# Block-sparse attention and rational FFN: weight remainders subtracted on VectorE instead of GpSimd, and unit factors in one operation

## The chip, the core and the metric

The program runs on one core of a Trainium2 chip. The metric is the device time of one execution in microseconds. Three runs of the kernel before took 829.0, 827.88 and 829.31 us; their median is 829.0 us. Engines are called as in the profile: PE is TensorE (matmuls), DVE is VectorE, ACT is ScalarE, POOL is GpSimd, SP is SyncE.

## The reference, cut to what matters

```
# attention: batch 4, 8 heads, 768 positions in 24 blocks of 32, head_dim 64; a query block sees its
# neighbours, the first and last block, and three sampled blocks
attn = softmax(where(mask, q @ k.T / 8, -1e9));  x = (attn @ v) as (3072, 512)
# feed-forward: 512 -> 2048 -> 512; the weights w_in and w_out come as float64
h = x @ w_in
P = a[0] + a[1]*h + a[2]*h**2 + a[3]*h**3
Q = 1 + abs(b[0])*abs(h) + abs(b[1])*h**2
out = (P / (Q + 1e-6)) @ w_out
```

## The kernel before, in words

Attention goes over parts (a batch and a pair of query blocks): scores on PE (tile `m`), maxima on DVE (L829), exponentials on ACT (L848), transposes of the weights on PE (L894), values on PE (`av`), and the result, scaled, as a float16 pair `xh`, `xl`. The feed-forward part takes 256 rows of x at a time (a chunk) and 256 of the 2048 hidden columns at a time (a unit): PE multiplies into `ph` (L1036 to L1038), ACT and DVE evaluate the rational function (`sq`, `tt`, `ab`, `rr`; L1043 to L1081) up to `gh` and `gl`, and PE multiplies these with w_out into `acc` (L1093 to L1099).

The weights come in double precision and are turned into pairs of low-precision numbers on the chip, in about the first 215 us. A piece of w_out is loaded (`wl`), converted (`dw`, helper line L154 on POOL, L150 on ACT), packed by three DVE instructions (L441, L444, L447), rounded to its high part `wo_h`, and its low part `wo_l` is the difference of both: L461, 16 pieces of 128x512. A piece of w_in takes the same three packing steps, then a scale (`dw<-wi,scw`), a rounding to float16, and its low part is again a difference: L519, 16 pieces. For each group of units four factors are computed (`fc`, L1010: the scale of the group times 1, |b0|, a1 and a3), by four small operations; there are 7 groups in the kernel, four of them in the stretch of the weights.

The order of all instructions on all engines is computed in Python before the program runs: each step is an `Op` with an engine (or several that it may use, in `among`), a price in ns, what it waits for, and a due time. `issue` repeatedly picks the step that can start first by these prices. Each engine then executes its list strictly in that order and waits for semaphores on the way, so a wait holds everything that stands behind it. Where PE would idle early on, `issue` puts in matmuls on an identity matrix (`fill`, L162).

A piece's rounding (`wo_h`, key "o") and conversion may go to ACT, POOL or DVE as the planner finds them free; a w_in remainder ("l") could go to POOL alone, a w_out remainder ("p") to POOL or DVE.

Of the kernel before, what the change touches and what calls it, by code (L numbers as in the profile page):

```python
# [24 lines left out]
def kernel(  # L25
# [27 lines left out]
    nc = tc.nc  # L53
# [233 lines left out]

    par = const.tile([P, 8], F32, name="par")
    absb = const.tile([P, 2], F32, name="absb")
    bias = const.tile([P, NB, NS], F32, name="bias")  # L290

    def load_small():
# [4 lines left out]
    def setup():  # L297
        nc.vector.tensor_scalar(out=ix, in0=samp[0:1].rearrange("p i (n w) -> p i n w", w=2)[:, :, :, 0],
                                scalar1=0, scalar2=NB - 1, op0=ALU.max, op1=ALU.min)
        nc.scalar.activation(out=absb, in_=par[:, 4:6], func=AF.Abs)  # L300

        sf = work[:, 2 * NR * NB:3 * NR * NB].rearrange("p (n i) -> p n i", n=NR)
        nc.vector.tensor_copy(out=sf, in_=samp.rearrange("p i (n w) -> p n i w", w=2)[:, :, :, 0])
        ii = work[:, 5 * NR * NB:5 * NR * NB + NB]
        nc.gpsimd.iota(ii, pattern=[[1, NB]], base=0, channel_multiplier=0, allow_small_or_imprecise_dtypes=True)
        dup = work[:, 3 * NR * NB:4 * NR * NB].rearrange("p (n i) -> p n i", n=NR)
        tmp = work[:, 4 * NR * NB:5 * NR * NB].rearrange("p (n i) -> p n i", n=NR)
        for r in range(NR):
            nc.vector.tensor_tensor(out=dup[:, r], in0=sf[:, r], in1=ii, op=ALU.subtract)
        nc.vector.tensor_tensor(out=dup, in0=dup, in1=dup, op=ALU.mult)  # L310
        nc.vector.tensor_scalar(out=dup, in0=dup, scalar1=1.0, scalar2=None, op0=ALU.is_le)
        for edge in (0.0, NB - 1.0):
            nc.vector.tensor_scalar(out=tmp, in0=sf, scalar1=edge, scalar2=None, op0=ALU.is_equal)
            nc.vector.tensor_tensor(out=dup, in0=dup, in1=tmp, op=ALU.max)
        for r in range(1, NR):
            for e in range(r):
                nc.vector.tensor_tensor(out=tmp[:, r], in0=sf[:, r], in1=sf[:, e], op=ALU.is_equal)
                nc.vector.tensor_tensor(out=dup[:, r], in0=dup[:, r], in1=tmp[:, r], op=ALU.max)
        nc.vector.memset(bias, 0.0)
        nc.vector.memset(bias[:, 1, NR:NR + 1], NEG)  # L320
        nc.vector.memset(bias[:, NB - 2, 1:2], NEG)
        for r in range(NR):
            for e in range(2):
                nc.vector.tensor_scalar(out=bias[:, 1 - e:NB:2, r + 5 * e], in0=dup[:, r, 1 - e:NB:2], scalar1=NEG, scalar2=None, op0=ALU.mult)
# [72 lines left out]
    def weights():  # L397
# [21 lines left out]
        def one(prio, kind, u, x, before):  # L419
            d = {}  # L420
            s_wl = Slot(r_wl) if kind else None
            s_w = Slot(r_dw) if kind else None

            def load():
                d["ld"] = early.tile([P, 2 * WC], I32, name="wl", bufs=2) if kind else raw(u, x)
                if kind:
                    nc.sync.dma_start(out=d["ld"], in_=wo64[x * P:(x + 1) * P])
                    return
                r0 = head(x, 0) * D
                if u == 0 and x == 0:  # L430
                    nc.gpsimd.tensor_copy(out=d["ld"][:, 0:1].bitcast(F32), in_=kall[:, 12, 0, 0:1])
                (nc.sync if u > 1 else nc.gpsimd).dma_start(out=d["ld"], in_=wi64[r0:r0 + P, u * 2 * WC:(u + 1) * 2 * WC])

            def convert(eng):
                d["w"] = early.tile([P, WC], I32, name="dw", bufs=3) if kind else wi[:, x, u].rearrange("p a n -> p (a n)").bitcast(I32)
                d["words"] = d["ld"].rearrange("p (n w) -> p n w", w=2)
                times(eng, d["w"].bitcast(F32), d["words"][:, :, 1].bitcast(F32), 2.0 ** -112)

            def pack1():
                w = d["w"]  # L440
                nc.vector.tensor_scalar(out=w, in0=w, scalar1=3, scalar2=None, op0=ALU.logical_shift_left)  # L441

            def pack2():
                nc.vector.scalar_tensor_tensor(out=d["w"], in0=d["words"][:, :, 0], scalar=29, in1=d["w"], op0=ALU.logical_shift_right, op1=ALU.bitwise_or)  # L444

            def pack3():
                nc.vector.scalar_tensor_tensor(out=d["w"], in0=d["words"][:, :, 1], scalar=-2 ** 31, in1=d["w"], op0=ALU.bitwise_and, op1=ALU.bitwise_or)  # L447

            def most():
                if u not in sums:  # L450
                    sums[u] = early.tile([P, 8], F32, name="sums")
                bound(d["w"].bitcast(F32), sums[u][:, x:x + 1])

            def out_high(eng):
                times(eng, wo_h[:, x], d["w"].bitcast(F32), 1.0)

            def out_short(eng):
                times(eng, wo_b[:, x], d["w"].bitcast(F32), 1.0)

            def out_low(eng):  # L460
                eng.tensor_tensor(out=wo_l[:, x], in0=d["w"].bitcast(F32), in1=wo_h[:, x].bitcast(F32), op=ALU.subtract)  # L461

            wl = [s_wl] if kind else []
            if kind or u > 1:
                o0 = Op(SY, [(475, 524288)], load, [o_setup] if kind else [freed[u - 1, x]], prio - 2, takes=wl, behind=before[kind])
            else:
                o0 = Op(PO, [(700, 524288)], load, [k_evac[0][3]] if u == 0 else [begun[0, x]], -17.0 + 1.2 * x if u else -84, behind=before[kind])
            before[kind] = o0
            w = [s_w] if kind else []
            o = Op(among("c", SC, sc=520, po=588, ve=335), 0, convert, [o0], prio, takes=w, uses=wl)  # L470
            if not kind:
                begun[u, x] = o
            o = Op(VE, 335, pack1, [o], prio, uses=w)
            o = Op(VE, 602, pack2, [o], prio, uses=wl + w)
            o = Op(VE, 602, pack3, [o], prio, uses=wl + w)
            if not kind:
                freed[u, x] = o
            if kind:
                o1 = Op(among("o", SC, sc=520, po=588, ve=335), 0, out_high, [o], prio, uses=w)
                o2 = Op(among("p", PO, po=1225, ve=602), 0, out_low, [o1] + homes(x), prio, uses=w)  # L480
                o3 = Op(among("q", SC, sc=520, po=588, ve=335), 0, out_short, [o] + homes(x), prio, uses=w)
                out_ready[x] = [o2, o3]
                decoded.append(o3)
                decoded.append(o2)
                return o2
            return Op(SC, 613, most, [o], prio)
# [9 lines left out]
    def w_scaled(u, prio, group, sums):  # L496
# [10 lines left out]
        for x in range(NCC):  # L507
            def three(x):
                d, s_ws = {}, Slot(r_dw)

                def scaled(eng):
                    d["w"] = early.tile([P, WC], I32, name="dw", bufs=3).bitcast(F32)
                    times(eng, d["w"], wi[:, x, u].rearrange("p a n -> p (a n)").bitcast(F32), sc[0])

                def high(eng):
                    times(eng, wi[:, x, u, 0], d["w"], 1.0)

                def low(eng):
                    eng.tensor_tensor(out=wi[:, x, u, 1], in0=d["w"], in1=wi[:, x, u, 0], op=ALU.subtract)  # L519

                a = Op(among("s", PO, po=671, ve=396, sc=613), 0, scaled, [o], prio, takes=[s_ws])
                a = Op(among("h", SC, sc=520, po=588, ve=335), 0, high, [a], prio, uses=[s_ws])
                a = Op(among("l", PO, po=1113, ve=602), 0, low, [a], prio, uses=[s_ws])
                in_ready.setdefault(u, []).append(a)
                decoded.append(a)
            three(x)
# [477 lines left out]
    def factors(b, u, n, after, prio):  # L1004

        def run():
            if b not in fcs:
                fcs[b] = p2.tile([P, 4, NU], F32, name="fc")
            for j, coef in enumerate((1.0, absb[:, 0:1], par[:, 1:2], par[:, 3:4])):
                nc.vector.tensor_scalar(out=fcs[b][:, j, u:u + n], in0=wscale[:, u:u + n], scalar1=v_inv[b], scalar2=coef, op0=ALU.mult, op1=ALU.mult)  # L1010
        for x in range(u, u + n):
            o_fc[b, x] = None
        o = Op(VE, 700, run, after + [o_fc.get((b, 0))], prio)
        for x in range(u, u + n):
            o_fc[b, x] = o

# [229 lines left out]
```

## Time and profile before

| | |
|---|---|
| median of three runs | 829.0 us |
| the profiled execution | 828.6 us, its span 826.8 us |
| PE busy | 770.6 us (93%) |
| DVE busy | 674.9 us (82%), 1580 instructions |
| ACT busy | 569.7 us (69%) |
| POOL busy | 107.5 us (13%), 149 instructions, all before 216 us |
| mean granted TensorE clock | 0.983 |

Busy time is the time in which at least one instruction of the engine is in execution. The span is the time from the first to the last instruction. The profile cuts the span into 40 slices of 20.7 us and gives the busy share of each engine in tenths:

```profile
PE   8798918898999999999999999999999999999997
DVE  2788999899988885788878884887888886887886
POOL 3547485613100000000000000000000000000000
PEclk9999969899999999999999999999999999999999
```

The sixth slice (103 to 124 us) is the one place where PE is nearly idle (1), and where its granted clock fell (6).

### The profile page before, as it was taken

What the parts mean: (1) busy time and instruction counts of PE and PEld (TensorE: products, weight loads), DVE (VectorE), ACT (ScalarE), POOL (GpSimd) and SP (SyncE); (2) the same over time, 40 slices, a digit from 0 to 9 for tenths busy, and PEclk for the clock granted to TensorE, in tenths of its full rate; (3) what the DMA queues carried; (4) which work ended last, traced back from release to release, by engine and by line L of the source; (5) the groups of instructions that cost most, each with busy time, mean ns of one, the idle gap of its engine ahead of it and who ended that gap; (6) DMA issues with size and microseconds to landing.
All of it is one profiled execution on the core that took longest, in us unless ns stands there. A gap on an engine that the chain in (4) does not pass through costs nothing.

```text
span 826.8 us, 27468 instructions
## 1 busy us (share of the span) xinstructions
PE 770.6 (93%) x10859; PEld 557.3 (67%) x10943; DVE 674.9 (82%) x1580; ACT 569.7 (69%) x1264; POOL 107.5 (13%) x149
## 2 busy tenths in 40 slices
PE   8798918898999999999999999999999999999997
PEld 4556605676677768677777767677777767767774
DVE  2788999899988885788878884887888886887886
ACT  2676777677866769677576759676676758766563
POOL 3547485613100000000000000000000000000000
PEclk9999969899999999999999999999999999999999
DMA  7988874537566957545636757635555436220000
GB/s 210 242 220 238 233 231 138 163 87 189 142 154 165 214 162 194 162 123 162 160 108 164 191 145 196 173 96 157 144 151 149 117 111 182 76 65 2 1 26 26
DMA packets 224416, 121.29 MB, mean 147 GB/s; under 512 B 62624, under 2 KB 214048, under 8 KB 224288
## 3 DMA queue, kind: packets, MB, share of 16 engines
q1 hardware_dynamic: 223136, 115.34, 51.6%
q0 software_dynamic: 1152, 4.19, 1.6%
q8 instruction: 86, 1.41, 0.8%
q14 instruction: 42, 0.34, 0.1%
HBM read 108.47 MB, written 11.01 MB: 145 GB/s over the span
## 4 chain that ended last, share of the span: by engine, by line
PE 81%; DVE 7%; DMA 4%; issue 3%; ACT 2%; POOL 2%; SPq 1%; ACTq 0%; POOLq 0%; DVEq 0%
PE acc L1093 11%; PE ph L1036 9%; PE acc L1095 9%; PE acc L1099 9%; PE ph L1037 9%; PE ph L1038 9%; PE m L817 7%; PE av L940 6%; PE m L894 6%; PE acc L162 3%; DMA vg<-in_v_dram 2%; PE m L556 2%; DMA wl<-in_moe_w_out_dram 1%; PE m L978 1%; POOL wo_h L154 1%
## 5 line engine op out<-in xcount | busy, mean ns | idle before, releaser
L1037 PE MATMUL ph<-xl,wi 128*128 128x256 f16 x768 | 210.5, 274 | 3.1 <-DVE xl L989 3.1
L1036 PE MATMUL ph<-xh,wi 128*128 128x256 f16 x768 | 210.9, 275 | 1.4 <-DVE tt L1053 1.4
L1038 PE MATMUL ph<-xh,wi 128*128 128x256 f16 x768 | 210.7, 274 | 0.0
L1043 ACT ACTIVATE sq<-ph,fc 128x512 f32<-128x512 f32 x96 | 65.9, 687 | 112.6 <-PE ph L1038 112.4
L1093 PE MATMUL acc<-wo_h,gh 128*128 128x512 f32 x384 | 114.5, 420 | 18.7 <-DVE gh L1071 18.0
L848 ACT ACTIVATE pr<-pr,st 128x256 f32<-128x256 f32 x224 | 110.7, 501 | 14.3 <-DVE st L860 14.3
L1060 DVE SCALAR_TENSOR_TENSOR ab<-sq,absb,ab 128x512 f32<-128x512 f32 x96 | 73.2, 763 | 37.1 <-ACT ab L1057 36.9
L829 DVE CUSTOM_DVE_ANT_1 pr<-m,bias 128x256 f32<-128x256 f32 x224 | 83.2, 418 | 22.3 <-PE m L817 22.1
L1099 PE MATMUL acc<-wo_b,gl 128*128 128x512 bf16 x368 | 95.4, 379 | 3.4 <-issue 2.1
L1095 PE MATMUL acc<-wo_l,gh 128*128 128x512 bf16 x316 | 86.5, 384 | 4.6
L1036 PEld LDWEIGHTS <-wi 128*128 128x128 f16 x768 | 75.9, 99 | 21.4 <-issue 5.1
L1071 DVE SCALAR_TENSOR_TENSOR gh<-tt,par,rr 128x512 fp32r<-128x512 f32 x96 | 72.3, 753 | 19.8 <-ACT rr L1067 11.2
L1093 PEld LDWEIGHTS acc<-wo_h,gh 128*128 128x128 f32 x384 | 66.0, 191 | 32.7 <-issue 19.6
L150 ACT ACTIVATE pT<-m 128x512 f32<-128x512 f32 x112 | 64.1, 596 | 34.0 <-PE m L894 32.7
L1037 PEld LDWEIGHTS <-wi 128*128 128x128 f16 x768 | 75.6, 98 | 12.7 <-issue 0.2
L1038 PEld LDWEIGHTS <-wi 128*128 128x128 f16 x768 | 75.5, 98 | 12.6 <-issue 3.4
L1047 ACT ACTIVATE tt<-ph,par,fc 128x512 f32<-128x512 f32 x96 | 74.8, 779 | 0.3 <-DVE gl L1081 0.2
L1050 DVE TENSOR_TENSOR tt<-tt,sq 128x512 f32<-128x512 f32 x96 | 66.9, 697 | 9.4 <-ACT tt L1047 9.4
L1057 ACT ACTIVATE ab<-ph,fc 128x512 f32<-128x512 f32 x96 | 65.6, 683 | 11.2 <-DVE tt L1077 10.5
L1077 DVE SCALAR_TENSOR_TENSOR tt<-tt,par,ab 128x512 f32<-128x512 f32 x96 | 72.2, 752 | 0.5
L894 PE MATMUL m<-ident,pr 128*128 128x128 f32 x448 | 69.6, 288 | 2.9 <-ACT kt L150 2.3
L1053 DVE SCALAR_TENSOR_TENSOR tt<-ph,fc,tt 128x512 f32<-128x512 f32 x96 | 71.4, 744 | 0.8
(130 smaller groups left out, 1221.7 us busy)
## 6 DMA issues: line engine op xcount, KB each, us to landing
vg<-in_v_dram SPq DMA_DIRECT2D x312, 64.0 KB, 2.9
vg<-in_v_dram SPq DMA_DIRECT2D x88, 192.0 KB, 3.6
kall<-ks SPq DMA_DIRECT2D x138, 64.0 KB, 1.9
wl<-in_moe_w_out_dram SPq DMA_DIRECT2D x16, 512.0 KB, 4.8
vg<-in_v_dram SPq DMA_DIRECT2D x12, 512.0 KB, 5.1
kall<-ks SPq DMA_DIRECT2D x23, 256.0 KB, 3.7
ldq<-in_q_dram SPq DMA_DIRECT2D x20, 256.0 KB, 3.4
out_dram<-ld SPq DMA_DIRECT2D x20, 256.0 KB, 2.4
```

Source lines behind the costliest of these rows:

```text
L829: nc.vector.tensor_tensor_reduce(out=prs[x][:, e, g].rearrange("p (s r) -> p s r", r=BLK), in0=h["sp"][g][:, e], in1=add.rearrange("p (s o ...
L848: nc.scalar.activation(out=prs[x][:, e, g], in_=prs[x][:, e, g], func=AF.Exp, scale=SCALE, bias=st[:, 12 + y:13 + y], accum_out=st[:, 16 + ...
L894: nc.tensor.transpose(pp[:, jj * P:(jj + 1) * P], pr[:, e, g, kt:NS * BLK:2], ident)
L1036: nc.tensor.matmul(o, wh, xh[:, :, cc], start=(cc == 0), stop=False)
L1037: nc.tensor.matmul(o, wh, xl[:, :, cc], start=False, stop=False)
L1038: nc.tensor.matmul(o, wl, xh[:, :, cc], start=False, stop=(cc == NCC - 1))
L1047: nc.scalar.activation(out=d["tt"], in_=d["ph"], func=AF.Identity, scale=d["cst"][:, 3:4], bias=par[:, 2:3])
L1060: nc.vector.scalar_tensor_tensor(out=d["ab"], in0=d["sq"], scalar=absb[:, 1:2], in1=d["ab"], op0=ALU.mult, op1=ALU.add)
L1071: nc.vector.scalar_tensor_tensor(out=d["gh"], in0=d["tt"], scalar=par[:, 0:1], in1=d["rr"], op0=ALU.add, op1=ALU.mult)
L1093: nc.tensor.matmul(acc, g, wo_h[:, f], start=(new and e == 0), stop=False)
L1095: nc.tensor.matmul(acc, g, wo_l[:, f], start=False, stop=False)
L1099: nc.tensor.matmul(acc, g, wo_b[:, f], start=False, stop=(last and e == 1))
```

## The change

The w_in remainder ("l") and the w_out remainder ("p") are given to DVE alone, priced at 602 ns each. The four small operations that make a group's factors become one `scalar_tensor_tensor` over four coefficients and n units; the four coefficients are gathered once, in the setup, into a tile `coefs` by a memset and three copies of one column, the first of which reads what ACT has just written (`absb`). The price of the step falls from 700 to 180 ns. Five lines are added, so that L461 of before is L466 after, L519 is L524, L441/L444/L447 are L446/L449/L452, and L1071 (`gh`) is L1076.

```
+    coefs = const.tile([P, 4], F32, name="coefs")
...
         nc.scalar.activation(out=absb, in_=par[:, 4:6], func=AF.Abs)
+        nc.vector.memset(coefs[:, 0:1], 1.0)
+        nc.vector.tensor_copy(out=coefs[:, 1:2], in_=absb[:, 0:1])
+        nc.vector.tensor_copy(out=coefs[:, 2:3], in_=par[:, 1:2])
+        nc.vector.tensor_copy(out=coefs[:, 3:4], in_=par[:, 3:4])
...
-                o2 = Op(among("p", PO, po=1225, ve=602), 0, out_low, [o1] + homes(x), prio, uses=w)
+                o2 = Op(among("p", VE, ve=602), 0, out_low, [o1] + homes(x), prio, uses=w)
...
-                a = Op(among("l", PO, po=1113, ve=602), 0, low, [a], prio, uses=[s_ws])
+                a = Op(among("l", VE, ve=602), 0, low, [a], prio, uses=[s_ws])
...
-            for j, coef in enumerate((1.0, absb[:, 0:1], par[:, 1:2], par[:, 3:4])):
-                nc.vector.tensor_scalar(out=fcs[b][:, j, u:u + n], in0=wscale[:, u:u + n], scalar1=v_inv[b], scalar2=coef, op0=ALU.mult, op1=ALU.mult)
+            nc.vector.scalar_tensor_tensor(out=fcs[b][:, :, u:u + n], in0=coefs.rearrange("p (j o) -> p j o", o=1).broadcast_to([P, 4, n]), scalar=v_inv[b],
+                                           in1=wscale[:, u:u + n].rearrange("p (o u) -> p o u", o=1).broadcast_to([P, 4, n]), op0=ALU.mult, op1=ALU.mult)
...
-        o = Op(VE, 700, run, after + [o_fc.get((b, 0))], prio)
+        o = Op(VE, 180, run, after + [o_fc.get((b, 0))], prio)
```

The whole order is planned anew with these prices. Counted over the program's order, DVE executes 32 remainders instead of 1, 7 factor operations instead of 28, and 7 fewer conversions, scalings and roundings (`dw<-wi,scw` 4 to 1, `dw<-wl` 2 to 0, `wo_h` 2 to 1, `wi<-wo_l` 2 to 1). POOL loses all of its 31 remainders and takes these 7 (43 operations of L154 instead of 36). ACT's number does not change, nor does the number of fill matmuls (135).

The first place is DVE's list where the first factors and the first `xl` are made (about 52 to 57 us of the trace before). Before:

```order
L344 TENSOR_REDUCE sc_1035<-m_101 128x1
L347 TENSOR_SCALAR sc_1035<-sc_1035 128x1
L351 TENSOR_SCALAR sc_1035<-sc_1035 128x1
L355 TENSOR_SCALAR sc_1035<-sc_1035 128x1
L356 TENSOR_SCALAR sc_1035<-sc_1035 128x1
L660 COPY xscale<-sc_1035 128x1
L1010 TENSOR_SCALAR fc<-wscale,sc_1035 128x2
L1010 TENSOR_SCALAR fc<-wscale,sc_1035,absb 128x2
L1010 TENSOR_SCALAR fc<-wscale,sc_1035,par 128x2 x2
```

After, the same stretch (`sc` is the scale of the values of the first batch, on which `xscale` and `xl` hang):

```order
L349 TENSOR_REDUCE sc_1040<-m_102 128x1
L524 TENSOR_TENSOR wi<-dw,wi 128x512
L352 TENSOR_SCALAR sc_1040<-sc_1040 128x1
L524 TENSOR_TENSOR wi<-dw,wi 128x512
L356 TENSOR_SCALAR sc_1040<-sc_1040 128x1
L524 TENSOR_TENSOR wi<-dw,wi 128x512
L360 TENSOR_SCALAR sc_1040<-sc_1040 128x1
L361 TENSOR_SCALAR sc_1040<-sc_1040 128x1
L971 TENSOR_TENSOR xn<-av,st 128x256
L665 COPY xscale<-sc_1040 128x1
L524 TENSOR_TENSOR wi<-dw,wi 128x512
```

The four remainders of the first group of w_in now stand between the steps of the scale; the single factor operation and both `xl` follow them.

The second place is DVE's list just ahead of the third `gh`, the one for which PE waited longest before. Before:

```order
L444 SCALAR_TENSOR_TENSOR dw<-wl,dw 128x512
L1050 TENSOR_TENSOR tt<-tt,sq 128x512
L447 SCALAR_TENSOR_TENSOR dw<-wl,dw 128x512
L1060 SCALAR_TENSOR_TENSOR ab<-sq,absb,ab 128x512
L1071 SCALAR_TENSOR_TENSOR gh<-tt,par,rr 128x512
```

After:

```order
L452 SCALAR_TENSOR_TENSOR dw<-wl,dw 128x512
L874 TENSOR_TENSOR st<-st 128x4
L452 SCALAR_TENSOR_TENSOR dw<-wl,dw 128x512
L877 TENSOR_SCALAR st<-st 128x4
L1055 TENSOR_TENSOR tt<-tt,sq 128x512
L880 RECIPROCAL st<-st 128x4
L466 TENSOR_TENSOR wo_l<-dw,wo_h 128x512
L1076 SCALAR_TENSOR_TENSOR gh<-tt,par,rr 128x512
L466 TENSOR_TENSOR wo_l<-dw,wo_h 128x512
```

Two w_out remainders stand now directly ahead of and behind this `gh`; the rounding `wo_h` that each of them needs is made on POOL.

The third place is POOL's list where it works on w_out pieces (101 to 122 us before). Before:

```order
L154 TENSOR_SCALAR wo_h<-dw 128x512
L461 TENSOR_TENSOR wo_l<-dw,wo_h 128x512
L154 TENSOR_SCALAR wo_h<-dw 128x512
L461 TENSOR_TENSOR wo_l<-dw,wo_h 128x512
L154 TENSOR_SCALAR dw<-wl 128x512 x2
L154 TENSOR_SCALAR wi<-wo_l 128x512
L461 TENSOR_TENSOR wo_l<-dw,wo_h 128x512 x2
L154 TENSOR_SCALAR dw<-wl 128x512
```

After:

```order
L154 TENSOR_SCALAR wo_h<-dw 128x512
L154 TENSOR_SCALAR wi<-wo_b 128x512
L154 TENSOR_SCALAR wo_h<-dw 128x512
L154 TENSOR_SCALAR dw<-wl 128x512
L154 TENSOR_SCALAR wo_h<-dw 128x512
L154 TENSOR_SCALAR dw<-wl 128x512
L154 TENSOR_SCALAR wo_h<-dw 128x512
L154 TENSOR_SCALAR dw<-wl 128x512
```

Nothing but operations with one input tensor is left on POOL there.

## Rows read from the trace of the kernel before

**Rows 1.** Busy time by stretch (us), instructions in brackets, clock, DMA.

```profile
core 0: us, PE busy (x) PEld busy (x) DVE busy (x) ACT busy (x) POOL busy (x), PEclk, DMA share, GB/s
50.00:225.00 175.00, 139.55 (x2342) 100.81 (x2352) 163.60 (x377) 126.85 (x288) 89.75 (x94) 0.92 0.64 180
109.60:126.60 17.00, 4.51 (x13) 2.81 (x14) 15.23 (x25) 11.23 (x26) 10.67 (x9) 0.50 0.63 204
225.00:800.00 575.00, 566.65 (x7658) 416.50 (x7728) 463.60 (x1068) 406.54 (x890) 0.00 (x0) 1.00 0.50 135
```

**Rows 2.** PE's waits, 46 to 230 us: us in total, times, longest.

```profile
PE acc L1093 <- DVE gh L1071: 18.0, 2, 17.6
PE ph L1037 <- DVE xl L989: 3.1, 1, 3.1
```

**Rows 3.** Chain of waits, 100 to 125 us: start, us, what.

```profile
101.42 7.89 POOL wo_h L154
...
109.39 1.58 POOL wo_l L461
...
121.28 0.67 DVE gh L1071
```

**Rows 4.** POOL's groups: count, busy us, mean ns, idle before.

```profile
L461 POOL TENSOR_TENSOR wo_l<-dw,wo_h 128x512 bf16<-128x512 f32 x15 | 22.5, 1503 | 13.5 <-ACT wo_h L150 11.7 <-DVE wo_h L152 1.1
L519 POOL TENSOR_TENSOR wi<-dw,wi 128x512 f16<-128x512 f32 x16 | 19.6, 1247 | 5.2 <-ACT wi L150 5.2
```

**Rows 5.** DVE in order of time: start, us, instruction, idle before it.

```profile
38.95 0.43 DVE L872 TENSOR_SCALAR st<-st 128x4 f32<-128x4 f32 x1
...
52.99 0.66 DVE L1010 TENSOR_SCALAR fc<-wscale,sc 128x2 f32<-128x2 f32 x1
...
101.98 0.42 DVE L441 TENSOR_SCALAR dw<-dw 128x512 int32<-128x512 int32 x1
102.31 0.68 DVE L1081 TENSOR_TENSOR gl<-tt,rr 128x512 bf16<-128x512 f32 x1
102.92 0.68 DVE L444 SCALAR_TENSOR_TENSOR dw<-wl,dw 128x512 int32<-128x512 int32 x1
...
109.76 1.75 DVE L444 SCALAR_TENSOR_TENSOR wi<-wo_b,wi 128x512 int32<-128x512 int32 x1
...
114.55 0.87 DVE L441 TENSOR_SCALAR dw<-dw 128x512 int32<-128x512 int32 x1 [1.77 <-POOL dw L154]
...
208.91 0.83 DVE L441 TENSOR_SCALAR dw<-dw 128x512 int32<-128x512 int32 x1
...
215.16 1.08 DVE L1077 SCALAR_TENSOR_TENSOR tt<-tt,par,ab 128x512 f32<-128x512 f32 x1
```

**Rows 6.** DVE in order of time at the third batch's factors.

```profile
398.86 0.23 DVE L1010 TENSOR_SCALAR fc<-wscale,sc 128x8 f32<-128x8 f32 x1
398.99 0.28 DVE L1010 TENSOR_SCALAR fc<-wscale,sc,absb 128x8 f32<-128x8 f32 x1
...
399.57 0.68 DVE L1074 SCALAR_TENSOR_TENSOR ab<-ab,gh 128x512 f32<-128x512 f32 x1
```

**Rows 7.** DVE's waits, 46 to 230 us.

```profile
DVE dw L154 <- POOL wi L519: 2.0, 1, 2.0
DVE dw L441 <- POOL dw L154: 2.0, 2, 1.8
DVE dw L154 <- POOL wo_l L461: 1.4, 1, 1.4
```

**Rows 8.** POOL in order of time: a rounding to `wo_h` that shares its time with DVE.

```profile
142.12 1.04 POOL L154 TENSOR_SCALAR wo_h<-dw 128x512 fp32r<-128x512 f32 x1
```

**Rows 9.** ACT's `absb`, then DVE in order of time, in the setup.

```profile
5.26 0.20 ACT L300 ACTIVATE absb<-par 128x2 f32<-128x2 f32 x1 [3.23 <-DMA par<-in_moe_b_dram]
...
4.54 0.26 DVE L303 CAST rr<-rr 128x72 f32<-128x72 int32 x1
...
11.65 0.69 DVE L152 COPY kall<-ph 128x512 f32<-128x512 f32 x1 [2.50 <-PE ph L556]
```

## The prediction

> **What bounds the kernel now.** I read the busy time by stretch first. From 225 to 800 us PE is busy 566.65 of 575 us at full clock; POOL does nothing there. From 50 to 225 us, while the weights are decoded, PE is busy for only 139.55 of 175 us and DVE for 163.60 [rows 1]. So whatever the change is worth, it is worth it before 225 us, and it reaches the end if PE, which has little air later, starts its steady part earlier or later by it.
>
> PE's waits say which engine ends its idle time there: 18.0 us for `gh` from DVE, of which one wait is 17.6, and 3.1 for `xl`, also from DVE [rows 2]. The chain of waits through that long wait runs over POOL, an engine that is 13% busy in the whole: a rounding to `wo_h` of 7.89 us, a remainder `wo_l` of 1.58, and at the end DVE's `gh` [rows 3]. The timeline of DVE shows why: at 109.76 an L444 took 1.75 us, while the one at 102.92 took 0.68, and POOL's remainder that began at 109.39 lay beside the long one; and at 114.55 DVE had been idle 1.77 us for a conversion on POOL [rows 3, 5]. I take from this that the two engines hold each other up, both ways: DVE's run of operations from 101.98 on kept POOL's 7.89 us operation waiting, and POOL's remainders lengthen DVE's.
>
> The Trainium skill has a rule for it ("SBUF — State Buffer", section "Who interferes with whom"): a DVE instruction with two SBUF inputs or in a two-port mode and a GpSimd instruction that reads SBUF exclude each other, and the later one is blocked for the whole of the earlier. These rows agree. By the rule alone the remainders could cost DVE up to their whole 42.1 us on POOL; the count below gives less than half of it, since DVE often had PSUM work or stood idle.
>
> **The change part by part.** All terms are DVE time between 50 and 225 us, where DVE is what PE waits for.
>
> Remainders: POOL loses 15 of 1503 ns and 16 of 1247 ns [rows 4], and DVE gains 31. On DVE a 128x512 operation on two tensors in SBUF takes its place in the list for 0.60 us: 102.31 to 102.92 is 0.61 [rows 5]. 31 x 0.60 = +18.6 us. Bound from below 0.60, and from above 0.75 each (+23) if the roundings beside them block some.
>
> What DVE gets back: I counted each DVE instruction that ran over 60 ns longer than the short value of its form, and put the excess down to the POOL instruction that overlapped it most. 27 belong to L461 and L519, the first at 52.99 and the last at 215.16 [rows 5], and sum to 19.4 us. 24 belong to POOL's 36 conversions, scalings and roundings (L154), the first at 38.95 and the last at 208.91 [rows 5], and sum to 9.6 us. So -19.4 from the remainders. Bounds: nothing, if other POOL work steps into the same places, and -19.4 - 9.6 = -29 if all of it goes.
>
> Moved conversions: DVE loses 7 of 0.33 us (101.98 to 102.31 [rows 5]): -2.3. POOL's L154 operations go from 36 to 43; at 9.6 / 36 = 0.27 us of DVE time each, 7 more cost +1.9.
>
> Factors: a group of four took 398.86 to 399.57 = 0.71 us where POOL was silent [rows 6]. The single operation over the broadcast coefficients is not in the trace; it lies between 0.13 us (the step from 398.86 to 398.99 [rows 6]) and 0.60 (a 128x512 one). With 8 elements a partition it is near the small one: 0.2. Four groups in this stretch: -0.5 x 4 = -2.0 (-0.4 to -2.3). Their blocked time is already in the 19.4. The three later groups stand where PE bounds: nothing.
>
> Setup: DVE must now wait for `absb`, which ACT ends at 5.46, instead of going on at 4.54, and does four small copies: some 1.3 us later. DVE then stands idle 2.50 us before the copy at 11.65 [rows 9]; that cover takes it. Without it the cost is 1.3.
>
> DVE's work together: 18.6 - 19.4 - 2.3 + 1.9 - 2.0 = -3.2 us.
>
> Waits that go: DVE waited 2.0 us for L519 and 1.4 for L461, and 1.8 for a conversion that stood behind remainders in POOL's list [rows 7]: -5.2.
>
> Waits that come: ten of the `wo_l` remainders on DVE need a `wo_h` that POOL makes. Where DVE's list between packing and remainder holds only work with its inputs in SBUF, as from 101.98 us on before, POOL may not get to start until DVE stops at the remainder. In DVE's list this is so, or nearly, for six of the ten. A rounding that shares its time with DVE takes 1.04 us [rows 8]; half of it, six times: +3.1. Bounds 0 and 10 x 1.04 = 10.4. Behind such a remainder stand `gh`, `ab` and `tt` of the next unit, and PE for them. The 16 w_in remainders wait for ACT's rounding; POOL waited 5.2 us in the same place [rows 4]. DVE has other work planned in between; I take +1.0, with 0 and 5.2 as ends.
>
> Sum: -3.2 - 5.2 + 3.1 + 1.0 = -4.3 us. The profiled execution took 828.6 us, of which the span is 826.8 and 1.8 lies around it; 828.6 - 4.3 = 824.3. The median of the runs is 829.0, 0.4 above it, so I put 824.5.
>
> **The rivals.**
>
> Ordered waits on DVE (slower). The remainders no longer sit in a queue of their own but in the list of the engine PE waits for, so each late rounding on POOL or ACT holds up the whole rational function behind it. For it: two remainders stand directly ahead of and behind the third `gh`, each behind a POOL rounding, and one such rounding took 7.89 us [rows 3]. Against it: when DVE stops, POOL has the memory to itself, so a wait ends within about 1 us. What I gain without any new wait is 3.2 + 5.2 = 8.4 us; from 8.4 us of waits on this is slower. At its ends, 10.4 + 5.2 = 15.6, it gives 828.6 + 7.2 = 835.8; in the middle between this and the turning point 832.
>
> A saturated engine (slower). The stall time is not given back, since other POOL work fills it, and only 18.6 - 2.3 - 2.0 = +14.3 remains: 843. The Trainium skill ("Perfetto Trace Analysis", section "Optimizing Scalar/DVE Operations") advises to move work from a saturated DVE to ScalarE or even GpSimd, the opposite of this change, but adds that between DVE and GpSimd it might not help, because they share a port. This trace bears out the second half: the 42.1 us on POOL cost DVE 19.4 plus 3.4 of waiting, more than the 18.6 that the same work costs there.
>
> No new waits (much faster). If DVE's list is such that the roundings are always ready, the 3.1 + 1.0 are not paid: -8.4. The clock may then stay up too: the stretch from 109.60 to 126.60 has a granted clock of 0.50, the lower of the two levels (1.2 GHz), having fallen while PE stood idle in its wait of 17.6 us, and PE is busy 4.51 us in it [rows 1, 2]; at 2.4 GHz half of this, 2.3, would come back: 828.6 - 8.4 - 2.3 = 817.9. Against it: the DVE work ahead of the third `gh` is hardly less than before, so PE idles there again.
>
> No change. PE's work is the same, and the relief of DVE may only lengthen its own idle time: 139.55 us of PE and 126.85 of ACT must also run through this stretch [rows 1]. Then 828 to 830. For it: the two orders run alike from the later batches on, where PE sets the pace. Against it: nearly all of PE's idle time before ends on DVE.
>
> **How the numbers follow.** A change of less than 0.2% (1.7 us) cannot be told from none here. Forecast, a gain of 2 to 9 us: 0.45. No new waits: 0.15. No change: 0.13. Ordered waits: 0.21. Saturated: 0.06. So faster 0.60, same 0.13, slower 0.27. The likeliest case alone reaches from 820 to 827; 8 in 10 lie between 815 and 834, which takes in most of the case without new waits and of the ordered waits.
>
> **What would show it.** If the step is right: DVE's busy time from 50 to 225 us is a few us lower or the stretch shorter by as much; L872, L441 and the two-input operations have means near those without POOL; 32 remainders on DVE at about 0.6 to 0.7 us; each `fc` operation near 0.2 us; PE's long wait for `gh` is there but some 4 to 6 us shorter; from 225 us on nothing differs. Wrong would be: DVE's waits on POOL's `wo_h` and ACT's `wi` together above 8 us (the ordered waits), or L154's means on POOL and DVE's excess beside them grown as much as the remainders' went (saturated). If the time falls below 818, the clock will show no low stretch near 110 to 127 us.

## The result, and the profile after

Four runs of the changed kernel have a median of 839.34 us, against 829.15 for four of the kernel before on the same chip: 1.0122 times, 95% interval 1.0106 to 1.0138. It is slower by 10 us; forecast were 824.5, and 834 as the upper end. The profiled execution took 839.82 us, its span 837.7.

The page of the changed kernel; busy time, then busy tenths in 40 slices of 20.9 us:

```profile
PE 783.8 (94%) x10943; PEld 559.9 (67%) x10943; DVE 668.2 (80%) x1587; ACT 570.9 (68%) x1264; POOL 65.3 (8%) x125
...
PE   7898755799899999999999999999999999999997
...
DVE  2688699889898886778877875787887886888886
...
POOL 3335134310000000000000000000000000000000
PEclk9999898699999999999999999999999999999999
```

POOL lost 42 us of busy time and DVE 7. PE's one empty slice (the 1 of before) has become four poor ones, 5 to 8, and the lowest clock stands two slices later. (The larger busy time of PE is not more work: the trace of before has 84 records of PE fewer.)

By stretch [rows 1]:

```profile
core 0: us, PE busy (x) PEld busy (x) DVE busy (x) ACT busy (x) POOL busy (x), PEclk, DMA share, GB/s
50.00:225.00 175.00, 138.83 (x2259) 97.61 (x2258) 152.10 (x376) 121.44 (x274) 47.69 (x70) 0.90 0.67 175
225.00:800.00 575.00, 572.93 (x7830) 417.14 (x7829) 462.60 (x1071) 410.40 (x902) 0.00 (x0) 1.00 0.57 137
```

DVE has 11.5 us more air in the stretch of the weights, and PE does no more in it, at a lower mean clock. The DMA engines are busier (0.67 for 0.64, and 0.57 for 0.50 later) at fewer or hardly more GB/s.

PE's waits, 46 to 230 us [rows 2]: what was waited for, us in total, times, longest.

```profile
PE m L344 <- ACT kt L150: 7.9, 1, 7.9
PE m L983 <- DVE st L834: 5.8, 1, 5.8
PE ph L1041 <- DVE tt L1058: 5.1, 4, 3.3
PE av L945 <- DMA vg<-in_v_dram: 4.8, 2, 3.5
...
PE m L561 <- DMA ldq<-in_q_dram: 1.8, 1, 1.8
PE acc L1098 <- DVE gh L1076: 1.3, 2, 1.0
```

The 17.6 us for `gh` are gone. In their place stand a wait of 7.9 for ACT, one of 5.8 for DVE, 3.3 for `tt`, and waits for two DMAs that before had none of this size. By the starts of the 96 `gh` operations, the changed kernel is 2.4 us late at the first (88 us before), between 5.1 and 11.1 from the second to the 16th, where the two orders differ, and between 10.3 and 10.7 from 248 us to 449. All of the loss arises before 248 us, and the steady part keeps its pace.

DVE's groups after [rows 4], then its waits, 46 to 230 us [rows 7]:

```profile
L466 DVE TENSOR_TENSOR wo_l<-dw,wo_h 128x512 bf16<-128x512 f32 x16 | 11.8, 737 | 1.3 <-POOL wo_h L154 1.3
L524 DVE TENSOR_TENSOR wi<-dw,wi 128x512 f16<-128x512 f32 x16 | 11.3, 726 | 2.2 <-ACT wi L150 2.1
L446 DVE TENSOR_SCALAR dw<-dw 128x512 int32<-128x512 int32 x16 | 6.9, 444 | 4.6 <-POOL dw L154 3.7 <-ACT dw L150 0.9
L1014 DVE SCALAR_TENSOR_TENSOR fc<-coefs,sc,wscale 128x8 f32<-128x8 f32 (+1 forms) x7 | 2.3, 323 | 0.0
```

```profile
DVE xn L971 <- PE av L945: 6.6, 4, 4.2
DVE pr L834 <- PE m L822: 6.2, 5, 2.4
DVE dw L446 <- POOL dw L154: 3.7, 2, 2.5
DVE wi L524 <- ACT wi L150: 2.1, 3, 0.9
DVE wo_l L466 <- POOL wo_h L154: 1.3, 3, 0.5
```

The remainders cost about what was forecast and hardly wait for their roundings. DVE now waits for PE, not PE for DVE alone. Nothing in DVE's own rows is worth 10 us, so the cause had to be looked for elsewhere.

Where PE first takes up a tile of q, in the setup. Before:

```profile
12.14 0.66 PE L556 MATMUL m<-ident,ldq 128*128 128x128 f32 x4
```

After:

```profile
14.22 0.66 PE L561 MATMUL m<-ident,ldq 128*128 128x128 f32 x4 [2.43 <-DMA ldq<-in_q_dram]
```

And the DMA row of the same time, what all queues moved in 40 slices of 0.4 us from 0 to 16 us. Before:

```profile
GB/s 0 0 0 0 30 49 49 37 17 8 62 194 291 286 285 273 287 270 207 210 261 289 286 263 271 235 260 284 271 277 228 108 13 0 96 96 165 180 236 353
```

After:

```profile
GB/s 0 0 0 0 29 50 49 35 17 11 58 204 288 287 255 217 218 218 207 223 222 199 213 228 227 220 219 215 219 219 219 231 168 158 122 179 201 184 236 297
```

Both start alike up to the 14th slice. Then the loads of k and q, which no edit touches, run at 263 GB/s before and 220 after, in the mean of the 15th to the 28th slice. The six tiles of k, 256 KB each in pieces of 256 bytes, land 0.91 us apart before (four of the five steps; one is 1.31) and 1.20 after (all five).

### The profile page after: what moved, and what is told of

Same layout as the page of the kernel before. It is cut to its first block, busy times and chain, and to the rows that moved or that the text cites. A ratio compares the mean times of both kernels' runs of the same rounds, so it can differ in the third digit from the quotient of the medians.

```text
span 837.7 us, 27545 instructions
## 1 busy us (share of the span) xinstructions
PE 783.8 (94%) x10943; PEld 559.9 (67%) x10943; DVE 668.2 (80%) x1587; ACT 570.9 (68%) x1264; POOL 65.3 (8%) x125
## 4 chain that ended last, share of the span: by engine, by line
PE 83%; DMA 5%; DVE 4%; SPq 2%; ACT 2%; issue 2%; POOL 1%; POOLq 0%; ACTq 0%; DVEq 0%
PE acc L1098 11%; PE ph L1041 10%; PE acc L1104 10%; PE acc L1100 10%; PE ph L1042 10%; PE ph L1043 10%; PE m L822 7%; PE av L945 6%; PE m L899 6%; DMA vg<-in_v_dram 3%; PE acc L162 2%; PE m L561 2%; PE m L983 1%; DMA ldq<-in_q_dram 1%; SPq L586 1%
## 5 line engine op out<-in xcount | busy, mean ns | idle before, releaser
L853 ACT ACTIVATE pr<-pr,st 128x256 f32<-128x256 f32 x224 | 110.7, 501 | 10.3 <-DVE st L865 10.3
L1100 PE MATMUL acc<-wo_l,gh 128*128 128x512 bf16 x384 | 101.2, 386 | 0.0
L1104 PE MATMUL acc<-wo_b,gl 128*128 128x512 bf16 x384 | 98.7, 379 | 2.0 <-DVE gl L1086 2.0
L1076 DVE SCALAR_TENSOR_TENSOR gh<-tt,par,rr 128x512 fp32r<-128x512 f32 x96 | 72.3, 754 | 20.9 <-ACT rr L1072 12.3
L1062 ACT ACTIVATE ab<-ph,fc 128x512 f32<-128x512 f32 x96 | 65.5, 683 | 13.4 <-DVE tt L1082 12.8
```

The lines of the kernel that those rows point to most:

```text
L853: nc.scalar.activation(out=prs[x][:, e, g], in_=prs[x][:, e, g], func=AF.Exp, scale=SCALE, bias=st[:, 12 + y:13 + y], accum_out=st[:, 16 + ...
L1076: nc.vector.scalar_tensor_tensor(out=d["gh"], in0=d["tt"], scalar=par[:, 0:1], in1=d["rr"], op0=ALU.add, op1=ALU.mult)
L1100: nc.tensor.matmul(acc, g, wo_l[:, f], start=False, stop=False)
L1104: nc.tensor.matmul(acc, g, wo_b[:, f], start=False, stop=(last and e == 1))
```

## The experiments

Theories at the start. T1: the remainders are cheaper on DVE, as forecast, and the order that is planned anew with their prices is at fault. T2: the remainders in DVE's list are at fault. T3: the setup's wait for `absb` delays the start. A fourth came from the DMA rows. T4: `coefs`, 16 bytes in a slot of 32, shifts all SBUF tiles behind it by 32 bytes, and loads to the shifted addresses are slower. In the built programs `tt` (k is loaded there first) lies at 153600 before and 153632 after, `vg0` at 114688 and 114720, `ldq` at 143360 and 143392: multiples of 256 before, 32 above one after.

Each ratio below is to the kernel before, run beside it on the same chip.

**ctrl: before, unchanged.**

> The kernel before, unchanged, profiled once more. It tells how far the first 50 us vary with nothing changed. In the profile before, the k tiles landed 0.9 us apart and PE idled 7.3 us in the first 50 us; in the changed kernel's profile 1.2 us apart and 10.6 us. If the start is a matter of the change (theory: the setup's wait for absb), this run lands the tiles 0.9 us apart again and PE idles 7 to 8 us; if it varies by itself, the steps lie between 0.9 and 1.2 us. Time 828 to 831 either way.

Measured: 828.55 us, 1.0003 (0.9989 to 1.0017). The same kernel under another name agrees within 0.2%.

**planB_dve: the order of before, the remainders executed by DVE.** The planner still takes them for POOL's; PE, ACT and SP have the lists of before word for word.

```
-                eng.tensor_tensor(out=wo_l[:, x], ...
+                nc.vector.tensor_tensor(out=wo_l[:, x], ...
-                    eng.tensor_tensor(out=wi[:, x, u, 1], ...
+                    nc.vector.tensor_tensor(out=wi[:, x, u, 1], ...
```

> The order of before on PE, ACT and SP word for word, and its factors; but the 31 remainders that stood in POOL's list are executed by DVE, at the place where the planner put them out. Theory 1 (the remainders are cheaper on DVE than the hold-ups they caused on POOL; the loss comes from the new order, in which PE's waits fall so that its clock is low while it works): faster than before by 2 to 7 us, 822 to 827. Theory 2 (the remainders in DVE's list hold up what stands behind them, whatever the order): slower than before by 5 to 12 us, 834 to 841.

Measured: 825.88 us, 0.9963 (0.9946 to 0.998), the first version that is faster, by 0.4%. DVE where before ran from 102.31 to 114.55 us [rows 5]:

```profile
101.51 0.69 DVE L461 TENSOR_TENSOR wo_l<-dw,wo_h 128x512 bf16<-128x512 f32 x1 [0.51 <-POOL wo_h L154]
102.12 0.68 DVE L1081 TENSOR_TENSOR gl<-tt,rr 128x512 bf16<-128x512 f32 x1
...
111.52 0.68 DVE L444 SCALAR_TENSOR_TENSOR wi<-wo_b,wi 128x512 int32<-128x512 int32 x1
...
113.38 0.41 DVE L441 TENSOR_SCALAR dw<-dw 128x512 int32<-128x512 int32 x1
```

Its longest wait of PE [rows 2], in the list of waits:

```profile
PE acc L1093 <- DVE gh L1071: 18.3, 2, 15.7
```

The L444 of 1.75 us now takes 0.68, and the L441 that stood idle 1.77 us for POOL does not wait (another L441, at 86.11 us, now waits 1.81 for a conversion on POOL; before it was 0.23); the remainder at 101.51 waits 0.51 us for its rounding; PE's wait falls from 17.6 to 15.7. T2 falls: in the same order the remainders are better off on DVE.

**planA_pool: the order of after, the remainders executed by POOL.** The same two lines in the changed kernel, with `nc.gpsimd`; the planner takes them for DVE's.

> The order of the changed kernel on PE, ACT and SP word for word, and its single factor operation; but the 32 remainders are executed by POOL at the place where the planner put them out. Theory 1 (the order is at fault): no better than the changed kernel, 839 to 848, since the hold-ups of DVE by POOL come back (some 19 us of DVE time). Theory 2 (DVE's list is at fault): near the kernel before, 827 to 833.

Measured: 840.43 us, 1.014 (1.0123 to 1.0157). All of the loss is there with no remainder on DVE.

**coefs_late: the four coefficient operations at the end of the setup.**

```
-        nc.vector.memset(coefs[:, 0:1], 1.0)
-        nc.vector.tensor_copy(out=coefs[:, 1:2], in_=absb[:, 0:1])
...
+        (the four lines as the last of setup)
```

> The changed kernel with the four operations that fill coefs moved to the end of the setup, so that DVE does not wait for absb at 4.5 us. Theory 3 (the setup's wait delays the start and with it everything): PE's first scores come 1 to 4 us earlier than in the changed kernel and the time falls by 1 to 4 us, 835 to 838. Theories 1 and 2: no change that can be told, 837.5 to 841.

Measured: 840.71 us, 1.0138 (1.01 to 1.0175). No gain, so T3 falls. The setup of the changed kernel, DVE in order of time [rows 9], says the same:

```profile
5.64 0.15 DVE L303 COPY coefs<-absb 128x1 f32<-128x1 f32 x1 [1.06 <-ACT absb L301]
...
11.40 0.69 DVE L152 COPY kall<-ph 128x512 f32<-128x512 f32 x1 [0.94 <-PE ph L561]
```

The wait of 1.06 us is there; the idle time before the copy shrinks from 2.50 to 0.94 and the copy stands no later than before.

**before_shift32: before, with an unused tile of 16 bytes.**

```
     absb = const.tile([P, 2], F32, name="absb")
+    pad = const.tile([P, 4], F32, name="pad")
```

> The kernel before, instruction for instruction, with one more 16-byte constant tile that nothing uses, allocated where the change puts coefs. It shifts the SBUF address of every tile behind it by 32 bytes, as coefs does: the k, q and v tiles (tt, ab, sq, ldq, vg) then no longer start at a multiple of 256 bytes. Theory 4 (the shifted addresses make these loads slower, and that is what costs the time): the k tiles land 1.2 us apart instead of 0.9, the median landing of the 64 KB v loads goes from 2.9 to 3.8 us, and the time rises by 6 to 12 us, to 835 to 841. Theory 1 (the new order is at fault): no change, 827 to 831.

Measured: 835.46 us, 1.0067 (1.0043 to 1.0091), with every instruction as in before. This shows that the shift alone costs 0.7%. By the starts of `gh`, this kernel is 8.0 us late at the first (88 us before) and 8.4 at 248 us, so nearly all of its loss arises in the first 88 us; from 248 to 803 us it loses 0.4 more. The engines' own work on the shifted tiles is no slower: from 225 to 800 us `gh` takes 747 ns in the mean before and 746 here, and the `sq` of the whole run 687 in both.

**after_pad: the changed kernel, `coefs` with 512 bytes.** The later tiles stand where before had them, modulo 256.

```
-    coefs = const.tile([P, 4], F32, name="coefs")
+    coefs = const.tile([P, 128], F32, name="coefs")[:, 0:4]
```

> The changed kernel, instruction for instruction, with coefs given 512 bytes a partition instead of 16, so that all tiles behind it have the offset to a multiple of 256 bytes that they had in the kernel before. Theory 4: the k tiles land 0.9 us apart again, and the time falls to 822 to 829. Theory 1: 837 to 841 as in the changed kernel, whatever the loads do.

Measured: 830.92 us, 1.0034 (1.0015 to 1.0053): of 1.22%, 0.88% go with the alignment alone. That is above T4's range and below T1's: the addresses are most of the loss, and a part of it stays with the order.

The pages of four kernels at this point, the queue of the loads (packets, MB, share of 16 engines' span) and the median us from issue to landing of the most frequent load of v; for the first two also that of the most frequent load of `kall`. Before:

```profile
q1 hardware_dynamic: 223136, 115.34, 51.6%
...
vg<-in_v_dram SPq DMA_DIRECT2D x312, 64.0 KB, 2.9
...
kall<-ks SPq DMA_DIRECT2D x138, 64.0 KB, 1.9
```

After:

```profile
q1 hardware_dynamic: 223136, 115.34, 56.6%
...
vg<-in_v_dram SPq DMA_DIRECT2D x312, 64.0 KB, 3.8
...
kall<-ks SPq DMA_DIRECT2D x138, 64.0 KB, 1.9
```

before_shift32:

```profile
q1 hardware_dynamic: 223136, 115.34, 57.4%
...
vg<-in_v_dram SPq DMA_DIRECT2D x312, 64.0 KB, 3.9
```

after_pad:

```profile
q1 hardware_dynamic: 223136, 115.34, 51.1%
...
vg<-in_v_dram SPq DMA_DIRECT2D x312, 64.0 KB, 2.9
```

The same packets and bytes; the pair shifted by 32 bytes keeps the DMA engines busy for a tenth more time, and a load of v lands 0.9 to 1.0 us later. The 256-byte packets of k and q that start between 5 and 12 us take 18 ns each in the median in before and after_pad, and 24 ns in the shifted pair. After 225 us this is hidden by PE's work. Ahead of that it is not: from 46 to 230 us PE waits 4.8 us for `vg` and 1.8 for `ldq` in the changed kernel, and 1.0 and nothing in after_pad. The loads of `kall` do not take part: 1.9 us, although that tile starts 32 bytes below a multiple of 256 before and on one after.

**planA_pool_pad: planA_pool with the 512 bytes.**

> The order of the changed kernel, with the remainders executed by POOL (840.4 us with shifted addresses), and coefs given 512 bytes. Theory 4: 826 to 834, some 3 us above the same with the remainders on DVE, as the hold-ups of DVE by POOL cost about that in the old order. Theory 1: 838 to 842.

Measured: 834.78 us, 1.0062 (1.0038 to 1.0086), just above T4's range. With it, seven of the eight corners of order, engine and addresses are measured (medians, us):

```
                              remainders on POOL   on DVE
order of before, aligned            829.0           825.9
order of after,  aligned            834.8           830.9
order of before, shifted            835.5           (not run)
order of after,  shifted            840.4           839.3
```

DVE instead of POOL is worth -3.1, -3.9 and -1.1 (the last lies within the noise: 1.0122 and 1.014 have overlapping intervals); the order of after costs 4.9 to 5.8; the shift costs 5.6 to 8.4. (The order of after comes with the single factor operation, that of before with four.) The way through the table from before to after is DVE -3.1, the order +5.0 and the shift +8.4.

**planB_aligned: planB_dve with two unused tiles, so that `kall` and the weights start on a multiple of 256 too.** In before `kall`, `wi`, `wo_h`, `wo_l` and `wo_b` lie 32 below one.

```
+    pad = const.tile([P, 4], F32, name="pad")
...
+    pad2 = const.tile([P, 120], F32, name="pad2")
```

> The order of before with the remainders on DVE (825.9 us), and two unused constant tiles that put kall and the weights, which the kernel before has 32 bytes below a multiple of 256, on such a multiple as well, with the k, q and v tiles left on one. Theory 4: the 256 KB loads of kall land in less than the 3.1 us before, and the raw loads of w_in into wo_l and wo_b sooner; the time falls by 0 to 4 us, 822 to 826. Theory 1: 825 to 827.

Measured: 824.56 us, 0.9943 (0.9923 to 0.9964), the fastest kernel of this study. Against planB_dve the intervals overlap, and the 256 KB loads of `kall` land no sooner (3.3 us against 3.1); that these last tiles matter is not shown.

Which part of the new prices spoils the order was open then, and three more were run: O1 says the remainders' place, O2 the factors' price of 180, O3 that any new plan is a new draw.

**lows_only: the remainders priced and executed on DVE, four factor operations, no `coefs`.**

```
-                o2 = Op(among("p", PO, po=1225, ve=602), ...
+                o2 = Op(among("p", VE, ve=602), ...
-                a = Op(among("l", PO, po=1113, ve=602), ...
+                a = Op(among("l", VE, ve=602), ...
```

> The kernel before with the remainders given to DVE in the planner (price 602 there) and executed by it; the four factor operations and the SBUF addresses as before. The changed kernel with the addresses put right took 830.9, and the order of before with the same engine for the remainders 825.9; which of the two edits of the planner's table spoils the order is open. If it is the remainders' place (O1), this takes 830 to 833 with PE at half clock for about 37 us. If it is the factors' price of 180 (O2), 825 to 827. If any new plan is a new draw (O3), it may lie anywhere from 824 to 836, and its sibling with the factors alone as well, with no sum of the two.

Measured: 828.25 us, 1.0003 (0.9984 to 1.0022).

**fc_only: the single factor operation, priced 180, `coefs` of 512 bytes; the remainders on POOL.**

> The kernel before with the single factor operation, priced 180 as in the change, coefs given 512 bytes so that the addresses keep their alignment; the remainders stay on POOL as before. O1 (the remainders' place spoils the order): the order is about as good as before, and the single operation saves DVE up to 2 us: 827 to 829.5. O2 (the price of 180 does): 833 to 836, as the order of after had with its remainders on POOL (834.8). O3 (a new draw): anywhere from 824 to 836.

Measured: 828.19 us, 1.0006 (0.9992 to 1.0021).

Neither shows the loss of both together (1.0034), though the intervals of both touch that of after_pad (1.0015 to 1.0053). O1 missed for lows_only (830 to 833) and hit for fc_only; O2 missed for both. O3 fits, but its range was so wide that it could hardly fail; which part of the prices makes the order of after worse stays open. The lows alone, planned anew, lose the 0.4% that they had gained in the old order (0.9963 to 1.0003).

**best: planB_aligned with the single factor operation, still priced 700**, `coefs` of 16 bytes in the place of `pad`.

> The order of before on every engine, the 31 remainders executed by DVE, the single factor operation in the place of the four (priced 700, so that the order stays), coefs of 16 bytes and a second unused tile of 480 bytes after wscale, so that loads land on the same addresses as in the aligned version of before's order (824.56). The single operation saves DVE 0.5 us four times before 225 us: 822.5 to 824.5 if DVE is what PE waits for there, 824.6 if it is not. Above 826 would mean that coefs, or the wait for it, costs something of its own.

Measured: 825.68 us, 0.9962 (0.9949 to 0.9975). That is above both outcomes expected, and below the 826 that would have shown a cost of `coefs`. The single operation brings nothing that can be seen beside planB_aligned; against before the gain of the remainders on DVE is confirmed.

**What the order costs PE.** In after_pad PE waits more often and shorter. A piece of it, in order of time:

```profile
118.95 0.47 PE L344 MATMUL m<-ident,sums 128*128 128x128 f32 x1 [7.18 <-ACT kt L150]
120.66 2.04 PE L1098 MATMUL acc<-wo_h,gh 128*128 128x512 f32 x4 [1.23 <-DVE gh L1076]
...
126.67 1.17 PE L1098 MATMUL acc<-wo_h,gh 128*128 128x512 f32 x4
```

The same four matmuls take 2.04 us after the wait and 1.17 later. The stretches of granted clock 0.50 before 225 us, of after_pad:

```profile
26.87:30.28 3.41, 3.27 (x55) 1.78 (x55) 2.07 (x11) 0.00 (x0) 1.24 (x4) 0.50 1.11 262
74.66:78.07 3.41, 3.04 (x30) 1.50 (x31) 2.10 (x4) 0.84 (x3) 1.48 (x3) 0.50 1.02 406
115.62:125.86 10.24, 5.68 (x17) 3.68 (x18) 9.33 (x24) 7.04 (x16) 4.30 (x5) 0.50 0.95 246
136.09:146.33 10.24, 5.80 (x26) 4.36 (x27) 9.86 (x34) 6.89 (x20) 1.30 (x2) 0.50 0.47 133
153.16:159.99 6.83, 5.28 (x28) 3.41 (x31) 5.94 (x10) 3.90 (x9) 0.00 (x0) 0.50 0.00 0
```

and of planB_dve:

```profile
107.14:124.21 17.07, 4.66 (x14) 2.95 (x15) 17.07 (x34) 12.35 (x28) 2.38 (x3) 0.50 0.73 228
141.27:148.10 6.83, 5.84 (x27) 4.21 (x28) 6.54 (x16) 4.51 (x10) 3.12 (x4) 0.50 0.46 127
```

PE does 23.1 us of its work at the lower level (1.2 GHz) in the one and 10.5 in the other. In planB_dve the clock is low mainly inside one long wait, where there is little to slow down. I summed for nine of the profiles PE's gaps of over 0.25 us before 230 us and half of its work at the lower clock:

```
                profiled us   gaps   half of work at 0.50   the rest
planB_dve          825.9      39.4          5.2              781.2
lows_only          825.8      37.3          9.4              779.1
fc_only            827.0      35.4         12.8              778.8
ctrl               827.3      39.1          9.0              779.3
after_pad          828.2      37.7         11.5              779.0
before             828.6      41.5          5.9              781.2
planA_pool_pad     836.4      43.8         14.6              778.0
before_shift32     837.6      46.5         12.2              778.9
after              839.8      46.5         13.4              779.9
```

The rest is the same within 3.2 us, while the time moves by 14. The two profiles of the unchanged kernel, before and ctrl, lie 3.1 us apart in clock and 2.4 in gaps, so differences of that size say nothing. The shift shows mostly as gaps (ctrl to before_shift32: 7.4 more, and 3.2 of clock), the order as clock with the remainders on DVE (planB_dve to after_pad: 6.3 more, and 1.7 less gaps) and as both with them on POOL (ctrl to planA_pool_pad: 5.6 of clock, 4.7 of gaps). The two columns put the order on DVE at 4.6 us, the medians at 5.0, but the rest falls by 2.2 and the two profiled executions lie only 2.4 apart: after_pad's was the fastest of its runs. And fc_only, as fast as before, has 12.8 of clock with the fewest gaps. So a low clock under work goes along with the new orders, but that it is what the order of after costs is argued, not shown: this is bookkeeping, and no run held the clock up in the new order.

## Why the prediction was wrong

The step that failed is the list of terms in the sum. It has terms for DVE's work and DVE's waits only, and puts two things at nothing that were worth more than all of it. The sum for the edits in themselves was about right.

- Not there: the addresses. It let the loads stay as they were and read `coefs` only as four small copies and a wait. The tile's 32 bytes slowed the loads of k, q and v and cost 5.6 to 8.4 us, the largest loss of all.
- Not there: the order. It priced the work and the waits of the new list as if the plan were as good as the old. The first and the second place that the order was quoted for show it moved; I looked there for new waits of DVE on roundings, not for what PE would be doing. Cost: 4.9 to 5.8 us; by which wait or which stretch of low clock stays open.
- Remainders, +18.6: in the changed kernel 737 and 726 ns in the mean, against 680 ns for a free one, so some 0.65 us in the list: 31 x 0.65 = 20. Right, within its bounds.
- Hold-ups given back, -19.4: none of DVE's long instructions lies beside a remainder any more. Right. The Trainium skill's rule ("SBUF — State Buffer", section "Who interferes with whom") agrees: with the remainders on DVE no second engine reads SBUF for them, and what is left beside POOL is the excess at L154.
- POOL's 7 more operations, +1.9: the excess beside L154 is 8.9 us after, 9.6 before. Too high by 2.6.
- Factors, -2.0: the single operation has a median of 246 ns over all seven (forecast 200), the four in the stretch of the weights took 217 to 551, and best shows no gain from it.
- The setup's wait hidden: right (coefs_late, and the copy at 11.40).
- Waits that go, -5.2: the two for remainders (3.4) went, that for POOL's conversion became 3.7 from 2.0. So -1.7.
- Waits that come, +3.1 and +1.0: 1.3 for `wo_h` and 2.1 for `wi`, together 3.4 for 4.1. Right in sum.
- PE's long wait 4 to 6 us shorter: in the old order 1.9 shorter; in the new one it was broken up.
- Nothing differs from 225 us on: right for the pace from about 250 us; the DMA engines were busier there too (0.57 for 0.50).

In the old order and at the old addresses, the only case in which the forecast's silent assumptions hold, the change of engine gave -3.1 us (0.9946 to 0.998), against -4.3 forecast for all edits. That this is so near is in part luck: in the changed kernel the waits that go were worth 3.5 us less than forecast and POOL's further operations cost 2.6 less. The time came out between the far end of the ordered waits, 835.8, and a saturated engine, 843, but the signs of both are missing. L154's hold-ups did not grow. The ordered waits would have needed 8 us of waits on roundings, and there are 3.4.

## What to carry to other kernels

A new small tile moves every tile behind it; before pricing the edit, compare the start addresses of all DMA targets, above all for loads that lay several short pieces side by side, and pad the tile if their alignment changes. When a planner makes the order, an edit of its prices is two changes: test the new engine with the old order first, and count a new order as a term of its own: the order of after cost 4.9 to 5.8 us, more than the edit gained, and none of the three new orders here was better than the old. Look also at what PE does in the stretches of low clock: with several middling waits it did 23.1 us of work at 1.2 GHz (after_pad), with one long wait 10.5 (planB_dve).

## What the runs showed of the hardware that was not expected

The loads of k, q and v slowed down when their target in SBUF started 32 bytes above a multiple of 256 instead of on one: 1.20 us instead of 0.91 for 256 KB of k, 220 GB/s instead of 263, 3.8 us instead of 2.9 to the landing of 64 KB of v. The pieces are 256 bytes for k and q and 512 for v, and eight of them lie side by side in a partition. The sources in HBM were the same. An unaligned start alone does not do it: the loads of `kall` of 64 KB, one piece of 512 bytes in each partition, land after 1.9 us both 32 bytes below a multiple of 256 (before) and on one (after). The loads of `xkg`, of the same shape, start 64 bytes above a multiple of 256 before and 96 above one after, and land after 1.9 and 2.0 us. What sets these loads apart from those of k, q and v, the eight pieces or something else, no run here isolates.

The Trainium skill ("DMA: Bandwidth & Descriptors", section "How a descriptor splits into AXI transactions") says that when a descriptor does not start on a multiple of 256 bytes, its first transaction starts at the boundary below, and says it of what is read. For k, q and v these runs agree in direction, for the side that is written: by its rule, as an estimate, a piece of 256 bytes that starts 32 above a multiple takes two transactions instead of one, and the measured time grew by 1.20 / 0.91 = 1.3. For `kall` they do not: the rule would give its pieces a further transaction too, and the 1.9 us show none.
